# Later weight requests for the last four experts, and other transfer sizes in the order model

## The chip, the core and the metric

The kernel runs on one NeuronCore of one Trainium2 chip. Its time is the device time of one execution in microseconds (us), from launch to end on that core; a time is the median of several executions. The engines are TensorE (PE; its weight loads are PEld), VectorE (DVE), ScalarE (ACT), GpSimd (POOL) and SyncE (SP). SP issues most transfers; POOL issues the indirect ones (gather, scatter) and the casting weight loads of the first three experts.

## The reference, cut to what matters

```python
# stage 1: retention, per batch b and head h (8 x 8, 576 positions, 64 wide)
scores = scale * q @ k.T ;  ret = scores * gamma[h] ** (i - j)   # for j <= i
x = (ret @ v) rearranged to (4608 tokens, 512)
# stage 2: noisy top-2 routing over 8 experts
noisy = x @ w_gate + log1p(exp(x @ w_noise)) * noise
top2, top2_w = the two largest of a token, softmax of the two
# stage 3: experts, 512 -> 1024 -> 512
for e in range(8):
    for k in range(2):
        rows = tokens whose k-th choice is e
        out[rows] += top2_w[rows, k] * (relu(x[rows] @ w1[e]) @ w2[e])
```

## The kernel before

**Staging.** Retention runs over 16 units, four to a pair of batches. When a pair is done, its tokens are routed (`route`), and their x rows, with gates and row numbers behind them, are stored to a DRAM table `xd` (line 1119). An expert's tokens stand in slots, up to 1216 of them (`CAP`), nine tiles of 128 rows and one of 64. A tile whose slots are filled by tokens of the first pairs of batches can be worked on early: `tiles` lists such early tiles (two slots each, `up`, line 1328), which go between the retention work; what is left are 19 late groups of up to four slots (`wide`, lines 1354 and 1418), worked one after the other, experts 0 to 7 in turn.

**One tile.** `fetch` gathers the 128 rows of a slot with one indirect transfer on POOL (line 1246, tile `xg`). Late groups are turned by a transposing transfer on SP (line 1258, `big<-xg`), early ones and those of expert 3 by TensorE (line 1268). Then come w1 (line 1354 or 1328), ReLU on ACT or DVE (lines 1337, 1339), w2 (line 1418; `halves`, line 1437, for the 64-row slot), the gate (lines 1471, 1473) and one or two scatters on POOL (line 1483): the first contribution to a row is written, the second is added in the transfer, or, where rows were read back before (`before`, line 1514, "held"), written too.

**Weights.** Each expert has eight parts of 512 KB: k = 0 to 3 are w1, 4 to 7 are w2. For experts 0 to 2 POOL loads them with a cast. For experts 3 to 7 SP loads each part as f32 into a `big` buffer (`part`, lines 1183 and 1186), and ACT or DVE casts it into the expert's place (lines 459, 461; `W<-big`, for expert 7 `xT<-big`, since it lies where `xT` lay). Experts 4 to 7 take the places of 0 to 3. They are asked for when the last late group of expert e-4 begins. `wide` counts steps, eight to a group; `due` releases the parts whose step has come, in the order in which they were listed, and looks at the head of the list alone.

```python
        for k in range(8):
            self.parts.append((self.step + SPREAD[e] * k, e, k))
```
```python
        while self.parts and self.parts[0][0] <= self.step:
            _, e, k = self.parts.pop(0)
```

**The order.** All operations are first recorded with costs (`pl.op`), and `Plan.run` then writes the order of each engine's instructions by a list schedule: it takes the operation with the earliest estimated start, in buckets of 0.05 us (line 351), then the one with the lower `prio`. The engines run in that order, each waiting on semaphores for real. The argument `dma` of an operation is the estimated occupation of the transfer path in us. It sets when a transfer is taken to have landed; a transfer of POOL also pushes the SP transfers behind it by as much.

```python
                if e == "SP":
                    x += o.dma / 0.95
                else:
                    x += o.dma / 0.85
                    if dma_free.get("SP", 0.0) > t + c:
                        dma_free["SP"] += o.dma
```

Between two indirect transfers of POOL in the estimated stretch from 85 to 200 us, a small memset is put in (line 444). Late gathers are additionally tied to TensorE's progress (`PACE`).

Of the kernel before, what the change touches and what calls it, by code (L numbers as in the profile page):

```python
# [27 lines left out]
NH = E * HPE  # L28
FIRST = (1216, 1024, 855, 690, 526, 361, 197, 0)
WAIT = (10, 15, 15)  # L30
SPREAD = (0, 0, 0, 0, 3, 3, 4, 4)
PACE = 2.343
REST = (85.0, 200.0, 1.6)
AHEAD = (2, 3)
# [379 lines left out]
class Kernel:  # L414
# [736 lines left out]
    def weights(self, e, prio, cast_dma, after=()):  # L1151
# [16 lines left out]
        for k in range(8):  # L1168
            self.parts.append((self.step + SPREAD[e] * k, e, k))
        self.due(prio, after)  # L1170
# [57 lines left out]
    def fetch(self, i, t, prio):  # L1228

        pl, nc = self.pl, self.nc  # L1230
        e, js, early = t
        ident = self.fixed["ident"]
        xi = self.fixed[f"xi{early}"]
        joint = [self.size(j) < P for j in js]
        xg = [self.tailx[e - 1] if two and e % 2 else pl.buf("xg", "exp") for two in joint]
        rows = 1 + 1152 * (early + 1)
        for x, j, two in zip(xg, js, joint):
            if two:
                if e % 2:
                    continue  # L1240
                self.tailx[e] = x
            h, n = HPE * e + j, P
            pace = PACE if early == 3 and i > self.ne else 0.0

            def get(_, x=x, h=h, n=n, pace=pace):
                ins = nc.gpsimd.indirect_dma_start(  # L1246
                    out=x.t[:n, :], out_offset=None, in_=self.xd[:rows, :], in_offset=IOff(ap=xi.t[:n, h:h + 1], axis=0),
                    bounds_check=rows - 1, oob_is_err=False)
                if pace:
                    self.tc.add_manual_dep(ins.ins, self.mm.ins.name, mybir.DependencyInfo(  # L1250
                        mybir.DependencyClass.Sync, mybir.DependencyReason.DATA), reason="gathers go at TensorE's pace")
            self.got = pl.op("POOL", 1.3, get, r=[xi if two else (xi, "m")] + self.xd_done[early], w=[x], prio=prio, dma=0.4, pace=pace, slack=3, ind=True, at="fetch1")
        xT = pl.buf("half" if early < 3 else "big", "xt")
        w, m, off = sum(self.size(j) for j in js), len(js) * P, self.off(js)
        xv = lambda m=m: xT.t.bitcast(BF16)[:, :KD * m].rearrange("p (k s) -> p k s", k=KD)
        if early == 3 and e != 3:
            for s, x in enumerate(xg):
                pl.op("SP", 2.0, lambda _, s=s, x=x, n=self.size(js[s]), p=self.span(e, js[s]): nc.sync.dma_start_transpose(
                    out=xv()[:, :, off[s]:off[s] + n], in_=x.t[p, :DM // 2].bitcast(BF16)),
                    r=[x], w=[(xT, s)], prio=prio, dma=1.1, hold=3, at="fetch2")  # L1260
        for c in range(0, 0 if early == 3 and e != 3 else len(js), 2):
            p = self.psum("xt")
            pv = lambda p=p: p.t.bitcast(BF16).rearrange("p (k s) -> p k s", k=KD)
            for s, x in enumerate(xg[c:c + 2]):
                def tr(_, a=off[c + s] - off[c], x=x, n=self.size(js[c + s]), q=self.span(e, js[c + s]), pv=pv):
                    xb = x.t[q, :DM // 2].bitcast(BF16)
                    for di in range(KD):
                        nc.tensor.transpose(pv()[:, di, a:a + n], xb[:, di * P:(di + 1) * P], ident.t[q, q])  # L1268
                pl.op("PE", 0.25, tr, r=[x, ident], w=[(p, s)], prio=prio, hold=5 if early == 3 else 0, at="fetch3")
            n = sum(self.size(j) for j in js[c:c + 2])  # L1270
            pl.op({"ACT": 0.2 + 0.0032 * n, "DVE": 0.15 + 0.00215 * n}, 0, lambda g, c=c, n=n, pv=pv: self.copy(
                g, xv()[:, :, off[c]:off[c] + n], pv()[:, :, :n]), r=[p], w=[(xT, c)], prio=prio + 2.25, at="fetch4")
        gi = []
        for x, j, two in zip(xg, js, joint):
            k = self.kind(e, j)
            pay = lambda x=x: x.t[:, DM // 2:]
            if early == 3 and two and e % 2 and e < 2:
                c = pl.buf("pay", "exp")
                pl.op("DVE", 0.1, lambda _, x=x, c=c: self.nc.vector.tensor_copy(c.t[:HD], x.t[HD:, DM // 2:DM // 2 + 3]),
                      r=[x], w=[c], prio=prio, hold=3, at="fetch5")  # L1280
                pay, x = (lambda c=c: c.t), c
            if k == "F":
                gi.append((lambda pay=pay: pay()[:, 0:1], lambda pay=pay: pay()[:, 2:3].bitcast(I32), None, x))
            elif k == "S":
                gi.append((lambda pay=pay: pay()[:, 1:2], None, lambda pay=pay: pay()[:, 2:3].bitcast(I32), x))
            else:
                gm, im = self.fix(f"gm{e}", [P, 1]), self.fix(f"im{e}", [P, 2], I32)
                m, mb = self.mix(e)
                V = nc.vector
                pl.op("DVE", 0.17, lambda _, pay=pay, gm=gm: V.tensor_tensor(  # L1290
                    gm.t, pay()[:, 1:2], pay()[:, 0:1], Alu.subtract), r=[x], w=[gm], prio=prio, hold=8, at="fetch6")
                pl.op("DVE", 0.17, lambda _, pay=pay, gm=gm, m=m: V.scalar_tensor_tensor(
                    gm.t, gm.t, m.t[:, 0:1], pay()[:, 0:1], Alu.mult, Alu.add), r=[x, gm, m], w=[gm], prio=prio, hold=8, at="fetch7")
                for y in range(2):
                    pl.op("DVE", 0.17, lambda _, pay=pay, im=im, mb=mb, y=y: V.tensor_tensor(
                        im.t[:, y:y + 1], pay()[:, 2:3].bitcast(I32), mb.t[:, y:y + 1], Alu.add),
                        r=[x, mb], w=[(im, y)], prio=prio, hold=8, at="fetch8")
                gi.append((lambda gm=gm: gm.t[:, 0:1], lambda im=im: im.t[:, 0:1], lambda im=im: im.t[:, 1:2], (gm, im)))
        self.t[i] = dict(xT=xT, xv=xv, gi=gi, w=w)
# [147 lines left out]
    def finish(self, i, t, s, prio, split=False):  # L1447

        pl, nc, tc = self.pl, self.nc, self.tc
        e, js, _ = t  # L1450
        d = self.t[i]
        j = js[s]
        g, first, second, src = d["gi"][s]
        src = list(src) if isinstance(src, tuple) else [src]
        po, n, q = d["po"][s], self.size(j), self.span(e, j, 2)
        y = d.get("y", {}).get(s)
        pair = n < P and e >= 2
        if pair and e % 2:
            y = self.taily[e - 1]
        held = y is not None and (not pair or e >= E - 2)  # L1460
        y = y or pl.buf("half", "exp")
# [29 lines left out]
        if first:  # L1491
            key = self.outk.setdefault(e, pl.fix())
            self.scats.setdefault(i, []).append(pl.op("POOL", 1.3, lambda _: scat(first, False), r=[y] + src, w=[(key, j)],
                                                      prio=prio, dma=0.76, ind=True, at="finish3"))
        if second:
            rd = [self.outk[x] for x in self.outk if x < e]
            self.scats.setdefault(i, []).append(pl.op("POOL", 1.3 if held else 1.8, lambda _: scat(second, not held),
                                                      r=[y] + src + rd, prio=prio, dma=0.9, after=self.reads if held else (), ind=True, at="finish4"))

    def before_it(self, e):  # L1500
        return [w for x in range(e) for w in self.firsts[x]]
# [1 line left out]
    def before(self, i, t, s, prio):  # L1503

        pl, nc, tc = self.pl, self.nc, self.tc
        e, js, _ = t
        q = self.span(e, js[s], 2)
        if self.size(js[s]) < P:
            q, e = slice(0, P), E - 1
        g, first, second, src = self.t[i]["gi"][s]  # L1510
        y = pl.buf("half", "ty")

        def get(_):
            ins = nc.gpsimd.indirect_dma_start(
                out=y.t[q, :], out_offset=None, in_=self.out[:, :], in_offset=IOff(ap=second()[q], axis=0),
                bounds_check=N - 1, oob_is_err=False).ins
            tc.declare_no_dep(ins, group="scat", keep=self.before_it(e), reason="rows of out are disjoint or ordered by hand")
            tc.add_to_no_dep_group("scat", ins)
        self.reads.append(pl.op("POOL", 1.3, get, r=[src] + [self.outk[x] for x in self.outk if x < e], w=[y], prio=prio - 2, dma=0.9))
        self.t[i].setdefault("y", {})[s] = y  # L1520


# [226 lines left out]
```

## Time and profile before

| | us |
|---|---|
| median of 3 runs | 412.27 (411.06 to 412.5) |
| profiled execution, whole | 412.69 |
| its span, first to last instruction | 411.1 |
| PE busy in the span | 377.1 |
| POOL busy | 291.0 |
| ACT busy | 272.3 |
| DVE busy | 148.2 |
| moved by transfers | 98.06 MB, mean 239 GB/s |

The profile is of one execution; times inside it count from the first instruction. In the windows view each row is a stretch, with the busy time and (in brackets) the number of instructions of PE, PEld, DVE, ACT and POOL, the TensorE clock granted (1.00 is full speed), the mean busy share of the 16 transfer engines and GB/s. In the timeline a row is start, duration, engine, line, operation and tiles; the square brackets give the idle time ahead of it and what ended it. A line with a q at the engine is its sequencer.

### The profile page before, as it was taken

To read this page: it belongs to the slowest core of one execution; us is meant where nothing else is said; L and a number is where in the kernel's file an instruction comes from. 1 tells how busy PE (TensorE), PEld (TensorE's weight loads), DVE (VectorE), ACT (ScalarE), POOL (GpSimd) and SP (SyncE) were. 2 spreads that over 40 slices of the span, in tenths; PEclk is the share of its full clock that TensorE was granted. 3 is DMA by queue.
4 is the path that set the end of the run, shared out by engine and by line. 5 is a ranking of instruction groups with operands and counts; after the bars stand their busy time and mean duration, and the time that the engine had idled before them with its cause. 6 is when DMAs were issued, how large, how long until landed. Compare 5 with 4: busy or idle time off the path is not lost.

```text
span 411.1 us, 11031 instructions
## 1 busy us (share of the span) xinstructions
PE 377.1 (92%) x4320; PEld 233.3 (57%) x4320; DVE 148.2 (36%) x413; ACT 272.3 (66%) x468; POOL 291.0 (71%) x379
## 2 busy tenths in 40 slices
PE   4998867889898898999999999999999999999994
PEld 2567656677575666767556554544554454454453
DVE  8456798788269587220111322101011000000002
ACT  2589978898787765776555877666686445555451
POOL 8676783990799848778676477778675776728564
PEclk9899999989999999999999999999999999999999
DMA  8999998999999989999989899999999998839766
GB/s 226 290 298 255 317 305 254 306 269 252 275 286 205 264 188 284 395 246 221 280 188 377 288 331 223 260 251 230 296 257 211 165 202 152 164 45 133 127 94 131
DMA packets 106184, 98.06 MB, mean 239 GB/s; under 512 B 40975, under 2 KB 83472, under 8 KB 106130
## 3 DMA queue, kind: packets, MB, share of 16 engines
q1 hardware_dynamic: 85858, 60.92, 56.0%
q0 software_dynamic: 17584, 36.24, 43.4%
q8 instruction: 34, 0.56, 0.6%
q10 hardware_dynamic: 2688, 0.18, 0.4%
q14 instruction: 20, 0.16, 0.2%
HBM read 73.11 MB, written 26.10 MB: 241 GB/s over the span
## 4 chain that ended last, share of the span: by engine, by line
PE 65%; DVE 8%; POOL 7%; DMA 6%; issue 6%; ACT 6%; POOLq 0%; SPq 0%; another core or an unknown queue 0%; DVEq 0%; ACTq 0%
PE ps L1418 25%; PE ps L1354 23%; PE ps L1328 6%; POOL out_dram L1483 4%; DMA xd<-xg 2%; ACT half L459 2%; DMA half<-in_v_dram 2%; DVE half L783 2%; PE ps L1437 2%; PE ps L808 2%; PE ps L467 1%; POOL half L721 1%; ACT xT L459 1%; DVE olo L1074 1%; PE ps L1268 1%
## 5 line engine op out<-in xcount | busy, mean ns | idle before, releaser
L1337 ACT ACTIVATE half<-ps 128x512 bf16<-128x512 f32 (+5 forms) x184 | 90.6, 503 | 87.5 <-PE ps L1354 55.0
L1418 PE MATMUL ps<-W,half 128*128 128x512 bf16 x432 | 137.8, 379 | 1.4 <-issue 1.1
L1354 PE MATMUL ps<-big,W 128*128 128x512 bf16 (+4 forms) x448 | 124.5, 326 | 0.6 <-DVE half L1473 0.6
L1246 POOL DMA_INDIRECT xg<-xd,xi x76 | 79.1, 1040 | 48.2 <-DMA half<-in_v_dram 11.7
L1483 POOL DMA_INDIRECT out_dram<-half,xg x71 | 90.3, 1272 | 30.1 <-issue 14.8
L1418 PEld LDWEIGHTS <-half 128*128 128x128 bf16 x568 | 54.5, 98 | 62.8 <-issue 3.1
L1354 PEld LDWEIGHTS <-W 128*128 128x128 bf16 x448 | 43.8, 98 | 33.4 <-issue 0.8
L1354 PE MATMUL ps<-big,xT 128*128 128x512 bf16 (+2 forms) x160 | 47.6, 337 | 0.0
L1471 ACT ACTIVATE half<-ps,xg 128x512 f32<-128x512 f32 (+1 forms) x58 | 39.3, 678 | 10.0 <-PE ps L1418 6.7
L783 DVE TENSOR_TENSOR half<-ps,mask 128x512 bf16<-128x512 f32 x64 | 40.3, 682 | 14.3 <-PE ps L775 10.9
L1418 PE MATMUL ps<-xT,half 128*128 128x512 bf16 x136 | 44.9, 379 | 0.0
L459 ACT ACTIVATE half<-ps 128x1024 bf16<-128x1024 bf16 (+1 forms) x42 | 38.5, 946 | 7.9 <-PE ps L744 4.0
L1473 DVE TENSOR_SCALAR half<-ps,xg 128x512 f32<-128x512 f32 (+1 forms) x17 | 10.6, 623 | 76.8 <-PE ps L1437 42.0
L1328 PE MATMUL ps<-half,W 128*128 128x256 bf16 (+1 forms) x288 | 29.1, 255 | 1.6 <-DVE half L461 0.8
L1339 DVE TENSOR_SCALAR half<-ps 128x512 bf16<-128x512 f32 (+5 forms) x12 | 6.8, 569 | 60.5 <-issue 32.9
L1328 PEld LDWEIGHTS <-W 128*128 128x128 bf16 x288 | 23.7, 98 | 5.8 <-issue 1.8
L467 PE MATMUL ps<-mask,ident__61 128*128 128x512 bf16 x68 | 20.3, 429 | 3.7 <-DVE hpf L527 3.7
L1469 DVE SCALAR_TENSOR_TENSOR half<-ps,xg,half 64x256 f32<-64x256 f32 (+2 forms) x7 | 3.6, 521 | 55.2 <-PE ps L1437 32.4
L1354 PEld LDWEIGHTS <-xT 128*128 128x128 bf16 x160 | 15.6, 98 | 12.8 <-issue 0.4
L459 ACT ACTIVATE tb<-ps 64x512 bf16<-64x512 f32 x32 | 18.9, 591 | 4.0 <-POOL half L721 1.9
L459 ACT ACTIVATE W<-big 128x1024 bf16<-128x1024 f32 x20 | 21.0, 1059 | 0.0
L808 PE MATMUL ps<-half,half 64*64 64x64 bf16 (+2 forms) x512 | 17.2, 213 | 1.7 <-ACT xT L459 1.6
(204 smaller groups left out, 517.0 us busy)
## 6 DMA issues: line engine op xcount, KB each, us to landing
big<-in_moe_w_dram SPq DMA_DIRECT2D x40, 512.0 KB
W<-in_moe_w_dram POOLq DMA_DIRECT2D x12, 512.0 KB
xd<-xg SPq DMA_DIRECT2D x16, 264.0 KB
W<-in_q_dram SPq DMA_DIRECT2D x16, 256.0 KB
big<-in_k_dram SPq DMA_DIRECT2D x8, 512.0 KB
big<-in_v_dram SPq DMA_DIRECT2D x8, 512.0 KB
big<-in_q_dram SPq DMA_DIRECT2D x16, 256.0 KB
W<-in_k_dram SPq DMA_DIRECT2D x6, 512.0 KB
```

The costliest lines, as they stand in the source:

```text
L459: self.nc.scalar.activation(out, in_, Act.Copy)
L467: self.nc.tensor.matmul(b.t, lhsT=ident, rhs=mask.rearrange("p r x -> p (r x)").unsqueeze(1).to_broadcast([P, 2, 2 * P]), start=True, stop ...
L783: nc.vector.tensor_tensor(S.t.bitcast(BF16).rearrange("p (h c x) -> p h c x", h=2, c=2)[:, h], p[h].t.rearrange("p (c x) -> p c x", c=2), ...
L808: nc.tensor.matmul(o[h * HD:(h + 1) * HD, hp, n, :], lhsT=kk[:k, r, c, y], rhs=vv[:k, r, c, y].unsqueeze(1).to_broadcast([k, n.stop - n.st ...
L1246: ins = nc.gpsimd.indirect_dma_start(out=x.t[:n, :], out_offset=None, in_=self.xd[:rows, :], in_offset=IOff(ap=xi.t[:n, h:h + 1], axis=0), ...
L1328: nc.tensor.matmul(pv()[:, f2, :], lhsT=w.t[:, o:o + P], rhs=xv()[:, di, :n], start=(di == 0), stop=(di == KD - 1))
L1337: self.nc.scalar.activation(o, i, Act.Relu)
L1354: self.mm = nc.tensor.matmul(p.t[:, :n], lhsT=w.t[:, o:o + P], rhs=xv()[:, di, :n], start=(di == 0), stop=(di == KD - 1))
L1418: self.mm = self.nc.tensor.matmul(po.t, lhsT=hv[:, c:c + P], rhs=self.W[e].t[:, o:o + DM], start=(f == 0), stop=(f == KF - 1))
L1471: nc.scalar.activation(y.t[q, c], x, Act.Copy, scale=g()[q])
L1473: nc.vector.tensor_scalar(y.t[q, c], x, g()[q], None, Alu.mult)
L1483: ins = nc.gpsimd.indirect_dma_start(out=self.out[:, :], out_offset=IOff(ap=ix()[q2], axis=0), in_=y.t[q2, :], in_offset=None, bounds_chec ...
```

## The change

`SPREAD` holds the number of steps between the parts of an expert. It goes from 3, 3, 4, 4 to 5, 6, 7, 8 for experts 4 to 7. Five estimates `dma` change: the gather from 0.4 to 0.3, the transposing transfer from 1.1 to 0.55, the scatter of first contributions from 0.76 to 0.55, the scatter of second contributions from 0.9 to 0.6 where rows were read back and to 1.2 where the transfer adds, the read-back from 0.9 to 0.6. No instruction is added or taken away by hand: the number of memsets between indirect transfers follows from the order.

```diff
-SPREAD = (0, 0, 0, 0, 3, 3, 4, 4)
+SPREAD = (0, 0, 0, 0, 5,6,7,8)
...
-            self.got = pl.op("POOL", 1.3, get, r=[xi if two else (xi, "m")] + self.xd_done[early], w=[x], prio=prio, dma=0.4, pace=pace, slack=3, ind=True, at="fetch1")
+            self.got = pl.op("POOL", 1.3, get, r=[xi if two else (xi, "m")] + self.xd_done[early], w=[x], prio=prio, dma=0.3, pace=pace, slack=3, ind=True, at="fetch1")
...
-                    r=[x], w=[(xT, s)], prio=prio, dma=1.1, hold=3, at="fetch2")
+                    r=[x], w=[(xT, s)], prio=prio, dma=0.55, hold=3, at="fetch2")
...
-                                                      prio=prio, dma=0.76, ind=True, at="finish3"))
+                                                      prio=prio, dma=0.55, ind=True, at="finish3"))
...
-                                                      r=[y] + src + rd, prio=prio, dma=0.9, after=self.reads if held else (), ind=True, at="finish4"))
+                                                      r=[y] + src + rd, prio=prio, dma=0.6 if held else 1.2, after=self.reads if held else (), ind=True, at="finish4"))
...
-        self.reads.append(pl.op("POOL", 1.3, get, r=[src] + [self.outk[x] for x in self.outk if x < e], w=[y], prio=prio - 2, dma=0.9))
+        self.reads.append(pl.op("POOL", 1.3, get, r=[src] + [self.outk[x] for x in self.outk if x < e], w=[y], prio=prio - 2, dma=0.6))
```

## Rows read from the trace of the kernel before

**Rows 1.** The page's parts 1 and 2: PE, then 40 slices of the span.

```profile
PE 377.1 (92%) x4320; PEld 233.3 (57%) x4320; DVE 148.2 (36%) x413; ACT 272.3 (66%) x468; POOL 291.0 (71%) x379
PEclk9899999989999999999999999999999999999999
DMA  8999998999999989999989899999999998839766
```

**Rows 2.** Windows of 20 us, four of the twenty-one.

```profile
100.00:120.00 20.00, 17.70 (x346) 12.94 (x344) 7.73 (x18) 15.78 (x28) 14.14 (x13) 1.00 1.10 290
...
180.00:200.00 20.00, 19.77 (x175) 13.43 (x173) 1.02 (x2) 12.28 (x22) 16.45 (x26) 1.00 0.99 242
...
220.00:240.00 20.00, 19.35 (x150) 11.91 (x148) 5.23 (x13) 14.22 (x26) 12.03 (x12) 1.00 0.93 335
...
380.00:400.00 20.00, 20.00 (x109) 10.09 (x108) 0.45 (x1) 9.91 (x19) 11.50 (x9) 1.00 0.72 108
```

**Rows 3.** Waits of PE from 200 us to the end: total, times, longest.

```profile
PE ps L1354 <- DVE half L1473: 0.6, 1, 0.6
```

**Rows 4.** The timeline around the last matmuls: PE, DVE and POOL.

```profile
403.76 1.92 PE L1427 MATMUL ps<-xT,half 128*128 128x256 bf16 x16
...
405.79 0.48 DVE L1469 SCALAR_TENSOR_TENSOR half<-ps,xg,half 128x256 f32<-128x256 f32 x1 [0.34 <-issue]
...
406.57 0.99 POOL L1483 DMA_INDIRECT out_dram<-half,xg  x1 [0.31 <-issue]
```

**Rows 5.** The timeline of POOL: four gathers, the first of all among them.

```profile
74.34 1.25 POOL L1246 DMA_INDIRECT xg<-xd,xi  x1 [0.17 <-DMA big<-in_q_dram]
...
105.14 1.11 POOL L1246 DMA_INDIRECT xg<-xd,xi  x1 [11.66 <-DMA half<-in_v_dram]
...
133.14 1.08 POOL L1246 DMA_INDIRECT xg<-xd,xi  x1 [0.31 <-issue]
...
149.62 1.08 POOL L1246 DMA_INDIRECT xg<-xd,xi  x1 [0.52 <-issue]
```

**Rows 6.** The timeline of PE: where late groups of experts 0, 4 and 7 begin.

```profile
199.02 0.92 PE L1354 MATMUL ps<-big,W 128*128 128x448 bf16 x4
...
268.57 0.38 PE L1354 MATMUL ps<-big,W 128*128 128x512 bf16 x1
...
369.58 0.38 PE L1354 MATMUL ps<-big,xT 128*128 128x512 bf16 x1
```

**Rows 7.** The timelines of DVE and ACT: first and last of 32 weight casts.

```profile
206.36 1.29 DVE L461 CAST W<-big 128x1024 bf16<-128x1024 f32 x2 [3.52 <-PE ps L1354]
...
315.33 1.05 ACT L459 ACTIVATE xT<-big 128x1024 bf16<-128x1024 f32 x1
```

**Rows 8.** The timeline of SP's queue: its longest piece with weight parts behind it.

```profile
286.83 15.70 SPq L1258 DMA_TRANSPOSE big<-xg  x4
```

**Rows 9.** Groups of POOL by line, 74 to 200 us: count, busy us, mean ns.

```profile
L1246 POOL DMA_INDIRECT xg<-xd,xi x29 | 30.1, 1039 | 20.8 <-DMA half<-in_v_dram 11.7 <-PE ps L1418 4.8 <-issue 3.8
L1483 POOL DMA_INDIRECT out_dram<-half,xg x15 | 15.3, 1021 | 3.3 <-issue 2.7 <-ACT xg L459 0.6
```

**Rows 10.** Windows of 5 us, six of those between 70 and 200 us.

```profile
80.00:85.00 5.00, 3.12 (x88) 2.40 (x86) 4.29 (x25) 4.33 (x8) 4.96 (x6) 0.99 1.10 308
85.00:90.00 5.00, 5.00 (x99) 4.27 (x92) 3.89 (x14) 4.25 (x8) 4.92 (x11) 0.67 1.12 274
...
105.00:110.00 5.00, 3.38 (x48) 2.31 (x47) 0.00 (x0) 4.10 (x6) 4.50 (x5) 1.00 0.98 248
...
130.00:135.00 5.00, 3.95 (x73) 2.08 (x71) 4.43 (x6) 3.00 (x7) 4.52 (x7) 1.00 1.08 237
135.00:140.00 5.00, 3.35 (x104) 2.39 (x101) 3.81 (x5) 3.62 (x6) 4.51 (x6) 1.00 1.19 264
...
160.00:165.00 5.00, 3.89 (x30) 2.12 (x27) 1.75 (x7) 1.58 (x3) 4.45 (x7) 1.00 1.06 391
```

**Rows 11.** Line 1258 from 150 us: durations min, median, max, first and last start.

```profile
L1258 SPq DMA_TRANSPOSE big<-xg x55: 1170/1248/6954, 173.3 to 358.0; - x55
```

## The prediction

> **What bounds the kernel now.** I read the page's first two parts, then the windows, then the waits of PE, and last the timelines of the places where they differ. PE is busy for 92% of the span, and its slices are nearly full in the second half [rows 1]. The windows cut the span into four pieces. Up to the first gather at 74.34 us [rows 5] nothing in the order depends on a changed estimate, so the order is the old one there. From 74.3 to 199.0 us, where the first late group begins [rows 6], retention, routing and early expert tiles share all engines; in the five windows from 100 to 200 us, the first and the last of which are shown, PE stands idle for 2.30 + 3.32 + 0.80 + 1.60 + 0.23 = 8.25 us [rows 2]. From 199 us to the end of the last matmul at 403.76 + 1.92 = 405.7 us PE is full: of ten windows from 200 to 400 us nine show 20.00, one 19.35 [rows 2], and the list of PE's waits has one entry, 0.6 us [rows 3]. Then a tail of 411.1 - 405.7 = 5.4 us follows: the last gating on DVE, one scatter of 0.99 us on POOL, and its landing [rows 4]. So the end is the first 199 us, plus 206.7 us of back-to-back matmuls, plus the tail. The change takes no matmul away. It can win or lose in the 125 us from 74 to 199, and hardly anywhere else.
>
> **Part 1, the weight parts.** The late groups have eight steps each; experts 0 to 3 have 1, 2, 2, 2 of them and the others 3, so experts 4 to 7 begin at steps 56, 80, 104 and 128. The rows give the scale: step 0 at 199.0, step 56 at 268.6, step 128 at 369.6 us [rows 6], so (268.6 - 199.0) / 56 = 1.24 us a step at first and (369.6 - 268.6) / 72 = 1.40 later. Expert 4's parts were asked for at steps 0 to 21, and will be at 0 to 35. The lists of experts 5, 6 and 7 begin at steps 16, 32 and 48, but a part waits until the head of the list goes. So expert 5 now has parts 0 to 3 at step 35, together with expert 4's last, and the rest at 40 to 58 (before: 21 to 37); expert 6 parts 0 to 3 at 58, the rest at 60 to 81 (before: 37 to 60); expert 7 parts 0 to 4 at 81, the rest at 88 to 104 (before: 60 to 76).
> A late part would stop PE, so I price the nearest case. A request takes its way through SP's queue, the transfer and the cast. The longest piece in SP's queue ahead of weight parts is 15.7 us of transposes that wait for gathers [rows 8]. The last of the 32 casts ends at 315.33 + 1.05 = 316.4 us [rows 7]; its request was at step 76, 268.6 + 20 x 1.40 = 296.6 us, so 20 us is the way with that piece on it, and I take 20 for each. Expert 4's last part: 199.0 + 35 x 1.24 + 20 = 262.4 us, used in the second step of its second group (step 65, 281 us). Expert 5's w1: 262.4, used at step 80, 302. Expert 6's w1: step 58, 271.4 + 20 = 291, used at step 104, 336. Expert 7's w1: step 81, 303.6 + 20 = 324, used at 369.6; its last part: step 104, 336 + 20 = 356, used after step 136, 381 us. The smallest margin is 19 us, before it was larger (the last cast was 53 us ahead of expert 7's first matmul).
> What it saves: the casts, 32 of some 1.05 us, mostly on ACT, lie further apart, and SP's transposes find fewer weight parts beside them. PE waits for neither today. So the part is worth 0; its bounds are the only PE wait there, 0.6 us, gained or, where a bunch of casts on ACT holds up a ReLU once, lost.
> The trace thus leaves room for a later request: 316.4 against 369.6 us [rows 6, 7]. The Trainium skill speaks against this edit (DMA: Bandwidth & Descriptors, Rules for kernel authors: issue a transfer early and wait for it late, so that its fixed cost lies beside other work). By that rule the time would grow by whatever a part comes late; with 19 us left it is 0 here too, and the trace agrees as long as no cast comes later than its first matmul.
>
> **Part 2, the estimate of the gather, 0.4 to 0.3, and of first scatters, 0.76 to 0.55.** No instruction changes, only places in the order. From 74 to 200 us POOL issues 29 gathers and 15 scatters [rows 9]. Each gather now pushes SP's estimated landings 0.1 us less, each such scatter 0.21 less, where SP has transfers under way. Order is decided in buckets of 0.05 us, so one gather is enough to swap two instructions. By the three gathers that open later rounds (105.14, 133.14, 149.62 us [rows 5]) 2, 8 and 10 gathers and at the last 4 scatters have gone by: shifts of 0.2, 0.8 and 10 x 0.1 + 4 x 0.21 = 1.84 us. A swap helps when it fills one of PE's holes and costs when it puts an instruction ahead of its transfer in a queue that runs in order. Gain: at most the four largest holes between 105 and 165 us, 1.62 + 1.05 + 1.65 + 1.11 = 5.4 us [rows 10]. Loss: at most each shift waited for on POOL and passed on in full, 0.2 + 0.8 + 1.84 = 2.8 us. Neither end is excluded by a row; I take 0 between them, since PE has other work at hand in most of these windows.
>
> **Part 3, the transposes, 1.1 to 0.55, and the late scatters and read-backs.** The 55 transposes are issued from 173.3 us on [rows 11] and serve the late groups, where PE is full. They are taken to land 0.58 us earlier each, the adding scatters 0.35 us later (0.3 / 0.85), held ones and read-backs 0.35 earlier. POOL and SP are on no PE wait in that piece, so 0, with 0.6 us either way as in part 1. At the end the last scatter follows the last DVE gating directly [rows 4]: nothing to gain; a scatter put in the wrong place ahead of it costs one issue, 0.99 us.
>
> **The sum.** Profiled execution 412.69 = span 411.1 + 1.6 around it. Parts 1, 2 and 3 add 0, so 412.7 for an execution like it; that one lies 0.4 above the median of 412.27. Forecast: 412.3.
>
> **The rivals.**
> *An order that stalls (slower).* The shorter estimates let a gather go on POOL ahead of its stored rows, and retention's multiplies behind it wait, then the matmuls that need them. Such a wait stands in the trace: POOL idle for 11.66 us ahead of the gather at 105.14 [rows 5], with a hole of 1.62 us in PE's window behind it [rows 10]. Against it: the shift there is only 0.2 us. It decides once the shifts of the later rounds reach PE in full, 2.8 us: 412.3 + 2.8 = 415.1. A hole has a second price: after the window from 80 to 85 us, in which PE stood idle for 1.88 us, the next shows a granted clock of 0.67, a mix of the full 2.4 GHz and of 1.2 [rows 10]; 5 us at 0.67 instead of 1.00 lose 1.65 us. One more such window makes 416.8. The Trainium skill (TensorE: Matmul & The Clock Gate, Part 1) says that idleness halves the clock until matmuls have run densely again; the trace agrees in this place, though the holes after 100 us left the clock at 1.00.
> *An order that fills (faster).* Early matmuls come up sooner and close more than half of those four holes, about 3 us: 409.3. For it: in that stretch 8.25 us of PE's time are empty and work for early tiles exists. Against it: the holes are ended by several releasers, not by one late instruction.
> *Transfers in each other's way (hardly faster).* If thinner weight traffic were the gain, it would have to show in PE from 200 us on: at most 0.6 us, 411.7. This lies within no change.
> *The change doesn't do what it says.* The head of the list holds the parts back, so four or five come together at steps 35, 58 and 81 and w1 is not spread at all. With the margins above this costs nothing: 412.3.
>
> **How the numbers follow.** A measurement of this kernel can tell about 0.5%, 2.1 us, from no change. Forecast with parts 1 and 3 at 0 and part 2 within 2 us: 0.36; the change not spreading: 0.05; thinner traffic: 0.03; together no change, 0.44. The order that stalls: 0.30, at 414.4 to 417. The order that fills: 0.26, at 407 to 410.2. The predicted time is the likeliest's, 412.3. For 8 in 10 the range goes down to 408.6, past the filling rival's 409.3 and short of the full 5.4, and up to 416.8, the stalling rival with its clock.
>
> **What the profile would show.** Part 1 is right if the casts reach to about 350 us and PE's waits after 200 us stay near 0.6; wrong if PE waits for a cast or an ACT instruction there. Part 2 is right if POOL's timeline is the same up to 74 us and the first late group begins within 2 us of 199.0; it is wrong by as much as that start moves. Part 3 is right if the piece from there to the last matmul is 206.7 us long again, and the tail 5.4. The prediction fails if a single swap delays routing and so every tile behind it, or if retention ends earlier and PE's holes close together.

## The result

On the chip of the first measurement the changed kernel takes 420.42 us in the median of 20 runs (412.43 to 424.8), the kernel before 411.74 (408.19 to 413.22). The ratio given with the result compares, for each kernel, the executions close to its fastest (within about 1.5%), and is 1.011, 95% interval 1.0072 to 1.0148; the changed kernel's times spread so far that its plain median stands 2.1% above. Slower, then: by 1.1 to 2.1%. On a second chip, with the kernel before on the same chip, the ratio was 1.0248 (1.019 to 1.0306).

The profiled execution of the changed kernel took 424.57 us, one of its longest, with a span of 422.9. Where the span grew, in 20 us windows (columns as in [rows 2]):

```profile
core 0: us, PE busy (x) PEld busy (x) DVE busy (x) ACT busy (x) POOL busy (x), PEclk, DMA share, GB/s
...
100.00:120.00 20.00, 19.47 (x406) 15.08 (x405) 7.34 (x15) 17.85 (x31) 13.34 (x12) 0.99 1.14 293
...
180.00:200.00 20.00, 19.49 (x169) 12.97 (x167) 2.07 (x4) 11.73 (x21) 17.08 (x26) 1.00 0.96 241
...
220.00:240.00 20.00, 20.00 (x152) 12.40 (x151) 3.05 (x9) 15.38 (x28) 13.49 (x14) 1.00 0.89 282
...
300.00:320.00 20.00, 17.92 (x90) 8.12 (x88) 2.98 (x8) 10.88 (x18) 12.73 (x11) 0.91 1.07 274
320.00:340.00 20.00, 13.02 (x62) 5.89 (x60) 0.00 (x0) 9.26 (x16) 8.34 (x8) 0.89 1.20 200
340.00:360.00 20.00, 20.00 (x113) 10.24 (x112) 0.97 (x2) 11.42 (x21) 12.68 (x11) 0.94 0.92 174
```

The stretch before the late groups is no longer than it was: from 100 to 200 us PE's idle time is 3.88 us in the five windows together (two of them shown), against 8.25, while from 60 to 100 us it is 10.10 against 8.04. The hole is between 300 and 340 us, where PE had none before, and the granted clock is below 1.00 there too. The first late group and the last matmuls:

```profile
197.97 0.92 PE L1354 MATMUL ps<-big,W 128*128 128x448 bf16 x4
...
415.16 1.92 PE L1427 MATMUL ps<-xT,half 128*128 128x256 bf16 x16
```

Against [rows 6] the late groups begin 1.05 us earlier; against [rows 4] they end 11.4 us later. The late piece is 415.16 + 1.92 - 197.97 = 219.1 us long, 12.4 more than the 206.7 of before. The waits of PE and of ACT in it (PE's answer to [rows 3]):

```profile
PE ps L1418 <- ACT half L1337: 7.0, 2, 3.5
PE ps L1354 <- ACT half L1337: 2.1, 1, 2.1
...
ACT xT L459 <- DMA big<-in_moe_w_dram: 12.5, 5, 7.4
ACT W L459 <- DMA big<-in_moe_w_dram: 6.9, 2, 6.7
```

PE waits 9.1 us for ReLUs on ACT (line 1337), and ACT waits 19.4 us for weight parts (line 459). Before, PE waited 0.6 us there [rows 3], so 8.5 of the 12.4 us are new waits. The rest, 3.9 us, fits the lower clock: at 0.91, 0.89 and 0.94 the three windows from 300 to 360 us would lose 20 x (0.09 + 0.11 + 0.06) = 5.2 us if PE were busy all through them, which is an upper estimate. In the timelines of ACT and PE both waits stand side by side:

```profile
299.10 0.68 ACT L1471 ACTIVATE half<-ps,xg 128x512 f32<-128x512 f32 x1
306.50 1.06 ACT L459 ACTIVATE W<-big 128x1024 bf16<-128x1024 f32 x1 [6.73 <-DMA big<-in_moe_w_dram]
307.47 0.53 ACT L1337 ACTIVATE half<-ps 128x192 bf16<-128x192 f32 x2
...
324.27 0.61 ACT L1337 ACTIVATE half<-ps 128x512 bf16<-128x512 f32 x1
332.32 1.06 ACT L459 ACTIVATE xT<-big 128x1024 bf16<-128x1024 f32 x1 [7.44 <-DMA big<-in_moe_w_dram]
333.28 0.58 ACT L1337 ACTIVATE half<-ps 128x512 bf16<-128x512 f32 x1
...
336.33 1.06 ACT L459 ACTIVATE xT<-big 128x1024 bf16<-128x1024 f32 x1 [1.90 <-DMA big<-in_moe_w_dram]
...
307.83 0.38 PE L1354 MATMUL ps<-big,W 128*128 128x512 bf16 x1 [2.08 <-ACT half L1337]
...
333.91 0.39 PE L1418 MATMUL ps<-W,half 128*128 128x512 bf16 x1 [3.43 <-ACT half L1337]
...
337.93 0.61 PE L1418 MATMUL ps<-W,half 128*128 128x512 bf16 x1 [3.54 <-ACT half L1337]
```

In ACT's written order the cast at 306.50 stands ahead of ReLUs. Its part has not landed, and ACT does nothing for 6.73 us, while the results of finished matmuls wait for their ReLUs; PE runs out of ReLUs and stops until 307.83. The same happens at 332.32 and, with a shorter wait, at 336.33. The weights themselves are in time: experts 6 and 7 need these casts tens of us later. SP's queue shows why the parts are late:

```profile
282.04 12.85 SPq L1258 DMA_TRANSPOSE big<-xg  x4
294.98 0.53 SPq L1186 DMA_DIRECT2D big<-in_moe_w_dram  x1
295.61 2.96 SPq L1258 DMA_TRANSPOSE big<-xg  x2
298.66 0.54 SPq L1186 DMA_DIRECT2D big<-in_moe_w_dram  x1
299.29 4.49 SPq L1183 DMA_DIRECT2D big<-in_moe_w_dram  x4
306.56 12.71 SPq L1258 DMA_TRANSPOSE big<-xg  x3
319.36 0.53 SPq L1186 DMA_DIRECT2D big<-in_moe_w_dram  x1
```

In the list of SP's waits from 200 us on, the largest entry is that of the transposes for their gathers:

```profile
SPq L1258 <- DMA xg<-xd,xi: 55.2, 19, 7.2
```

Transposes hold SP for 12.85 us and for 12.71 us, and the parts are issued behind them. Before, a piece of 15.70 us stood in that queue [rows 8], and ACT waited for no part: new is where the casts stand. And a part that is issued does not land at once: by the order of the two queues, the part issued at 294.98 is the one that the cast at 306.50 waits for, 11.5 us, and that of 319.36 the one of the cast at 332.32, 13 us. In the order model a part's estimate is 1.35 / 0.95 + 2.16 = 3.6 us from issue to landing, and more only if the model has other transfers ahead of it.

### The profile page after: what moved, and what is told of

Its sections match the earlier page's. It is cut to its first block, busy times and chain, and to the rows that moved or that the text cites. A ratio compares the mean times of both kernels' runs of the same rounds, so it can differ in the third digit from the quotient of the medians.

```text
span 422.9 us, 11023 instructions
## 1 busy us (share of the span) xinstructions
PE 382.2 (90%) x4319; PEld 238.5 (56%) x4319; DVE 146.8 (35%) x410; ACT 275.5 (65%) x471; POOL 289.2 (68%) x376
## 5 line engine op out<-in xcount | busy, mean ns | idle before, releaser
L1418 PE MATMUL ps<-W,half 128*128 128x512 bf16 x432 | 140.2, 384 | 7.0 <-ACT half L1337 7.0
L1354 PE MATMUL ps<-big,W 128*128 128x512 bf16 (+4 forms) x448 | 127.1, 332 | 2.1 <-ACT half L1337 2.1
L1471 ACT ACTIVATE half<-ps,xg 128x512 f32<-128x512 f32 x58 | 39.7, 685 | 12.3 <-PE ps L1418 11.4
L783 DVE TENSOR_TENSOR half<-ps,mask 128x512 bf16<-128x512 f32 x64 | 40.3, 683 | 17.4 <-PE ps L775 13.6
L1473 DVE TENSOR_SCALAR half<-ps,xg 64x256 f32<-64x256 f32 (+1 forms) x17 | 10.1, 593 | 88.2 <-PE ps L1437 40.5
L459 ACT ACTIVATE W<-big 128x1024 bf16<-128x1024 f32 x22 | 23.1, 1053 | 7.0 <-DMA big<-in_moe_w_dram 6.9
L459 ACT ACTIVATE xT<-big 128x1024 bf16<-128x1024 f32 x16 | 16.7, 1054 | 13.1 <-DMA big<-in_moe_w_dram 13.0
L459 ACT ACTIVATE xg<-ps 128x1024 bf16<-128x1024 bf16 (+1 forms) x19 | 17.3, 940 | 6.3 <-PE ps L1110 5.4
```

The lines of the kernel that those rows point to most:

```text
L459: self.nc.scalar.activation(out, in_, Act.Copy)
L783: nc.vector.tensor_tensor(S.t.bitcast(BF16).rearrange("p (h c x) -> p h c x", h=2, c=2)[:, h], p[h].t.rearrange("p (c x) -> p c x", c=2), ...
L1354: self.mm = nc.tensor.matmul(p.t[:, :n], lhsT=w.t[:, o:o + P], rhs=xv()[:, di, :n], start=(di == 0), stop=(di == KD - 1))
L1418: self.mm = self.nc.tensor.matmul(po.t, lhsT=hv[:, c:c + P], rhs=self.W[e].t[:, o:o + DM], start=(f == 0), stop=(f == KF - 1))
L1471: nc.scalar.activation(y.t[q, c], x, Act.Copy, scale=g()[q])
L1473: nc.vector.tensor_scalar(y.t[q, c], x, g()[q], None, Alu.mult)
```

## Experiments

Theory C, made from this profile: a cast in ACT's order ahead of its part is what PE pays for. Its rival E: the hole comes with the order of the early stretch, or with this chip. All ratios are to the kernel before on the same chip; its median was 418.36 on the first of the three chips used, 410.95 on the second, 420.06 on the third, so times of different chips are not set against each other. Ratios of different chips are no close comparison either: the kernel after itself had 1.011 on one and 1.0248 on another. The first four runs were on the first chip.

**The new `SPREAD` alone.**

```diff
 # kernel before
-SPREAD = (0, 0, 0, 0, 3, 3, 4, 4)
+SPREAD = (0, 0, 0, 0, 5,6,7,8)
```

> The kernel before with the new SPREAD and the old estimates. Theory C (casts: a weight part asked for later stands in SP's queue behind transposes that wait for gathers, its cast stands in ACT's queue ahead of the ReLUs, and PE waits for these): slower than before by 2 to 9 us, with ACT waiting on DMA at line 459 for several us after 280 us and PE waiting for ACT line 1337. Theory E (the estimates alone make the difference, by the order of the stretch from 74 to 199 us): within 1 us of before, no such wait.

Ratio 1.0009 (0.998 to 1.0038): no change. No PE wait at all is listed after 199 us, no wait of ACT on a part, and the late piece is 205.6 us long. Theory C as written is wrong: later requests alone do not put a cast ahead of its part. Its chain of waits stays possible, with another start.

**The estimates alone.**

```diff
 # kernel after
-SPREAD = (0, 0, 0, 0, 5,6,7,8)
+SPREAD = (0, 0, 0, 0, 3, 3, 4, 4)
```

> The kernel after with the old SPREAD (3, 3, 4, 4). Theory C: the late piece is 207 us long again with under 1 us of PE waits, and the first late group begins about 1 us before 199.0 as in the profile after: 0 to 2 us faster than before. Theory E: slower than before by the 4 us or so that the changed kernel lost.

Ratio 0.9974 (0.9929 to 1.002). But in the waits of PE and ACT of this kernel, the old `SPREAD` notwithstanding:

```profile
PE ps L1354 <- ACT half L1337: 2.5, 1, 2.5
PE ps L1418 <- ACT half L1337: 1.2, 2, 0.9
...
ACT xT L459 <- DMA big<-in_moe_w_dram: 14.2, 4, 5.6
ACT W L459 <- DMA big<-in_moe_w_dram: 2.7, 2, 1.7
```

The late piece is 410.60 + 1.92 - 199.25 = 213.3 us. The estimates bring the waits, which neither theory said together with a level ratio. The twelve times reach from 414.05 to 425.55 us, and their median, 421.39, is 0.7% above that of the kernel before. Whether something else in the estimates gains is not shown by this run.

**The casts later in the order.**

```diff
 # kernel after, in part()
-        pl.op({"ACT": 1.06, "DVE": 0.7}, 0, lambda g: self.copy(g, w.t[:, k * F:(k + 1) * F], t.t), hold=1,
+        pl.op({"ACT": 1.06, "DVE": 0.7}, 0, lambda g: self.copy(g, w.t[:, k * F:(k + 1) * F], t.t), hold=14,
```

> The kernel after, but the order takes a weight part's cast for possible 14 us after its landing (hold 14 in place of 1), so that it stands later in ACT's queue; the requests are as in the kernel after. Theory C: ACT no longer waits on DMA at line 459, PE's waits after 200 us fall from 9 us to under 2, and the time is 411 to 413. If the late transfers themselves were the cause (a part that lands after its first matmul), PE would wait on the casts instead and nothing is won.

Ratio 1.0148 (1.01 to 1.0196): against the expectation, and not what was meant to be tried. The edit also holds for the casts of expert 3, which are loaded ahead of the others; PE lost 7.5 us in the one window from 200 to 220 us, and the late groups began at 210.81. In the late piece, 418.92 + 1.92 - 210.81 = 210.0 us, the waits are fewer but not gone: from 210.8 us on PE waits 2.5 us for ReLUs on ACT, and ACT 8.2 us for parts. So 14 us of room in the model did not keep every cast behind its part here. The time tells nothing of the cause; the run with expert 3 left out of the edit stands below.

**The casts of experts 4 to 7 on DVE.**

```diff
 # kernel after, in part()
-        pl.op({"ACT": 1.06, "DVE": 0.7}, 0, lambda g: self.copy(g, w.t[:, k * F:(k + 1) * F], t.t), hold=1,
+        pl.op({"ACT": 1.06, "DVE": 0.7} if e < 4 else {"DVE": 0.7}, 0, lambda g: self.copy(g, w.t[:, k * F:(k + 1) * F], t.t), hold=1,
```

> The kernel after, with the casts of experts 4 to 7 on DVE alone, which is idle for over 85% of that piece. Theory C: a cast that waits for its part then holds up no ReLU on ACT; PE's waits after 200 us fall under 2 us and the time is 410 to 413. What could go on: DVE holds ReLUs and gatings too, which then wait behind the cast (PE waits for DVE lines 1339 or 1473).

Ratio 0.9904 (0.9865 to 0.9944). The thirteen times reach from 412.36 to 426.67 us, with a median of 417.12 against 418.36. The profile is of the longest: there DVE waits 88 us for parts, and PE 3.2 us for DVE's gating (line 1473) and 3.6 us for a transpose, where under 2 us had been expected. So in that execution the stall moved to another engine, and most of it cost PE nothing. What the shorter ones waited for is not known.

**The estimate of the transposes alone** (this and the next three on the second chip). Theory T: the transposes' 0.55 makes the order model take SP's queue for shorter than it is. Rival S: the estimates of gathers and scatters do it.

```diff
 # kernel before, in fetch()
-                    r=[x], w=[(xT, s)], prio=prio, dma=1.1, hold=3, at="fetch2")
+                    r=[x], w=[(xT, s)], prio=prio, dma=0.55, hold=3, at="fetch2")
```

> The kernel before with one change: the estimate of the transposing transfer 0.55 in place of 1.1. The order up to the late groups is that of before. Theory T (this one estimate makes the order model take SP's queue for shorter than it is, so that casts go into ACT's queue ahead of their parts): ACT waits on DMA at line 459 for 5 us or more, PE for ACT in the late piece for 2 us or more, and the time is 1 to 5 us above before. Theory S (the estimates of gathers and scatters do it): as before within 1 us and no such wait.

Ratio 1.018 (1.0128 to 1.0232), from five executions: one number makes the kernel slower. The order up to the late groups is that of before. Waits in the profiled execution, which at 411.45 us is the shortest of the five (the others 416 to 421):

```profile
PE ps L1418 <- ACT half L1337: 1.7, 1, 1.7
PE ps L1437 <- ACT half L1337: 0.8, 1, 0.8
...
ACT xT L459 <- DMA big<-in_moe_w_dram: 13.2, 4, 6.2
```

Its late piece is 402.40 + 1.92 - 195.77 = 208.6 us, 3.0 more than in the run with the new `SPREAD` alone. The waits are shown by this, but not all of the 1.8%: no profile of a longer execution of this kernel exists.

**The kernel after with the transposes at 1.1** (called transposes_old below)**.**

```diff
 # kernel after, in fetch()
-                    r=[x], w=[(xT, s)], prio=prio, dma=0.55, hold=3, at="fetch2")
+                    r=[x], w=[(xT, s)], prio=prio, dma=1.1, hold=3, at="fetch2")
```

> The kernel after, with the estimate of the transposing transfer back at 1.1; SPREAD and the other estimates as in the kernel after. Theory T: PE's waits in the late piece fall under 1 us, and what is left is the gain of the order in the stretch from 74 to 199 us: 0 to 4 us faster than before. Theory S: the waits of 9 us stay.

Ratio 0.9945 (0.9916 to 0.9974). All other parts of the change are in it, `SPREAD` too, and it is faster than before. PE has no wait after 199 us, ACT waits for one part, and the late piece is 400.93 + 1.92 - 197.26 = 205.6 us:

```profile
197.26 0.92 PE L1354 MATMUL ps<-big,W 128*128 128x448 bf16 x4
...
400.93 1.92 PE L1427 MATMUL ps<-xT,half 128*128 128x256 bf16 x16
...
ACT xT L459 <- DMA big<-in_moe_w_dram: 0.8, 1, 0.8
```

Theory T holds, and S falls: gathers and scatters at their new estimates make PE wait for nothing.

**The estimates of gathers, scatters and read-backs alone.**

```diff
 # kernel after
-SPREAD = (0, 0, 0, 0, 5,6,7,8)
+SPREAD = (0, 0, 0, 0, 3, 3, 4, 4)
...
-                    r=[x], w=[(xT, s)], prio=prio, dma=0.55, hold=3, at="fetch2")
+                    r=[x], w=[(xT, s)], prio=prio, dma=1.1, hold=3, at="fetch2")
```

> The kernel before with the new estimates of gathers, scatters and read-backs alone (transposes 1.1, SPREAD 3, 3, 4, 4). Theory T: no wait of PE for casts, and the early order of the kernel after: 1 to 4 us faster than before. Theory S: ACT waits on casts as in the run with the estimates alone.

Ratio 0.9982 (0.9947 to 1.0017), no PE wait, late piece 205.6 us. ACT does wait 7.1 us for parts, in eight waits of at most 1.3 us; short waits on ACT cost PE nothing here. The expected gain is not beyond doubt here, and it overlaps with the run before it: whether `SPREAD` helps once the transposes are at 1.1 stays open.

**The kernel after once more.**

> The kernel after, on the same chip as these. By theories T and S alike 1.011 of before, with PE waits in the late piece of 5 to 10 us; a ratio of 1.00 would say that the first measurement was of that chip.

Ratio 1.0248 (1.019 to 1.0306). PE waits 8.2 us for ACT, ACT 17.4 for parts; the late piece is 215.8 us. The loss is no matter of the chip of the first measurement. Nor are the waits a matter of one long execution: this profile is of 419.29 us, where the five lie between 418.35 and 424.45.

**The casts of experts 4 to 7 later** (this and the last three on the third chip).

```diff
 # kernel after, in part()
-        pl.op({"ACT": 1.06, "DVE": 0.7}, 0, lambda g: self.copy(g, w.t[:, k * F:(k + 1) * F], t.t), hold=1,
+        pl.op({"ACT": 1.06, "DVE": 0.7}, 0, lambda g: self.copy(g, w.t[:, k * F:(k + 1) * F], t.t), hold=1 if e < 4 else 14,
```

> The kernel after, all its estimates and its SPREAD, but the casts of experts 4 to 7 alone are taken for possible 14 us after landing (hold 14 in place of 1); the early casts of expert 3 keep their place. Theory T: the place of the casts in ACT's queue is the cause; ACT's waits on DMA at line 459 fall under 3 us, PE's in the late piece under 1.5 us, and the time is 0.99 to 1.00 of before. If the waits go to other places (transposes, or PE waiting for a cast), the late requests themselves are to blame and the time stays above 1.01.

Ratio 0.987 (0.9797 to 0.9942), where the kernel after had 1.011 and 1.0248 on other chips. The five times reach from 412.68 to 427.50 us, with a median of 415.83 against 420.06, so the size of the gain is not firm. All estimates and the late requests are as in the kernel after; the late casts alone stand further back, all 32 of them on ACT. The waits of PE after 199 us, complete:

```profile
PE ps L1418 <- issue: 0.3, 1, 0.3
PE ps L1418 <- ACT half L1337: 0.2, 1, 0.2
```

ACT has no wait on a part, and the late piece is 206.2 us. So the place of the casts in ACT's order is the cause of the waits, and in this profile the later weights cost nothing.

**The gather's estimate alone.**

```diff
 # kernel before, in fetch()
-            self.got = pl.op("POOL", 1.3, get, r=[xi if two else (xi, "m")] + self.xd_done[early], w=[x], prio=prio, dma=0.4, pace=pace, slack=3, ind=True, at="fetch1")
+            self.got = pl.op("POOL", 1.3, get, r=[xi if two else (xi, "m")] + self.xd_done[early], w=[x], prio=prio, dma=0.3, pace=pace, slack=3, ind=True, at="fetch1")
```

> The kernel before with the gather's estimate alone at 0.3. Theory O (what is gained comes from the order of the stretch from 74 to 199 us, which this estimate already changes at the same instruction of PE as the whole change): 0 to 2.5 us faster than before, late piece within 1.5 us of 205.6. If the scatters' estimates do it: as before within 1 us.

Ratio 0.9899 (0.9857 to 0.994), the late piece 404.61 + 1.92 - 200.02 = 206.5 us. It is as long as before, so what this number gains should lie ahead of the late groups. That is argued: no profile of the kernel before on this chip exists, and all four kernels tried on it came out 1.0 to 1.5% below, so that the kernel before may just have been slow there. In PE's order it moves the same first instruction as the whole change does: four transposes of an early tile (line 1268) come in between retention's matmuls of line 775, earlier than they did.

**Requests that are really spread.**

```diff
 # kernel after with the transposes at 1.1, in weights()
-        self.due(prio, after)
+        self.parts.sort(); self.due(prio, after)
```

> As the run transposes_old, with the list of due parts sorted by step, so that each expert's parts really come 5, 6, 7 or 8 steps apart and none waits for the head of the list. If bunched requests cost something: up to 1 us faster than transposes_old, 0.990 to 0.9945 of before. If they cost nothing: 0.9945 within 0.003. A late piece of 205.6 us without PE waits is the floor, and no more than that can come from it.

Ratio 0.9899 (0.9828 to 0.997), with a median of six of 418.93 against 420.06; and the waits are back: ACT 11.7 us for parts, PE 3.5 us for ACT, a late piece of 210.1 us. With the bunches (transposes_old) there were none, so it is not the bunches that bring the waits. Sorting asks for every part at its own step, so for the w1 of experts 5 to 7 earlier than with the bunches; why casts then stand ahead of their parts again is open.

**A little room for each cast.**

```diff
 # kernel after with the transposes at 1.1, in part()
-        pl.op({"ACT": 1.06, "DVE": 0.7}, 0, lambda g: self.copy(g, w.t[:, k * F:(k + 1) * F], t.t), hold=1,
+        pl.op({"ACT": 1.06, "DVE": 0.7}, 0, lambda g: self.copy(g, w.t[:, k * F:(k + 1) * F], t.t), hold=1 if e < 4 else 4,
```

> As the run transposes_old, with casts of experts 4 to 7 taken for possible 4 us after landing in place of 1. In the profile of transposes_old ACT waited 0.8 us on a part and PE for nothing, so 0.9945 of before within 0.003; if executions without a profile lose time to such waits now and then, it is faster by up to 1 us and its runs lie closer together.

Ratio 0.9855 (0.9812 to 0.9898), the fastest on its chip by the median, 414.30 against 420.06; no wait of PE after 199 us, none of ACT on a part, late piece 205.6 us. This version beats the kernel before. Against the kernel after, which was not run on this chip, only the ratios speak, 0.9855 against 1.011 and 1.0248.

## Why the prediction was right and wrong

The measured time lies in the range when the ratio 1.011 is taken (411.7 x 1.011 = 416.3, range 408.6 to 416.8); the plain median, 420.4, does not. The likeliest case, no change, did not come about, and the slower time came by a mechanism that was not the slower rival's. So it is luck that the range holds 416.3: its upper end was made from a stall on POOL that did not happen.

- *What bounds the kernel: right, in the main.* The late piece is matmuls back to back and has a floor: 205.6 us in four kernels with the one `SPREAD` or the other and several sets of estimates. "Hardly anywhere else" was wrong: a piece with nothing to gain had 9 us to lose.
- *Part 1, `SPREAD`: right by itself, for half of the reason given.* 0 was forecast and 1.0009 measured. The margins held: no kernel shows PE waiting on a late weight part in the late piece, but for 0.6 us for a cast in the kernel with the list sorted. The step that failed is the next sentence: that PE waits for neither, "so the part is worth 0", bounds 0.6 us. I priced a cast that comes too late for its matmul. I did not price a cast that stands too early in an in-order queue, and what is queued behind it; the bunch of casts on ACT was named, at 0.6 us where the profile shows 9.1. The sum also takes the parts as independent, and they may not be: PE's waits for ACT are 0 with the new `SPREAD` alone, 4.0 us with the estimates alone, and 9.1 and 8.2 with both, in single profiles.
- *Part 3, the transposes: the step that failed.* It gave 0 with 0.6 us either way, since POOL and SP were on no PE wait. But the estimate does not act on the transposes alone: it sets when the model takes the weight parts behind them in SP's queue for landed, and with that the place of their casts. Alone it has a ratio of 1.018, and back at 1.1 it takes the kernel after to 0.9945 without any PE wait. The 20 us from request to cast that I had read from [rows 7, 8] was the warning: the model allows 3.6 us from issue to landing for a part with nothing ahead of it. The old 1.1 was too long for one transpose, if the new figures are right, and too short for the queue's real waits; it had left room by accident. That last sentence is a reading, not a measurement.
- *Part 2, the early order: the right mechanism, on the other side of 0.* 0 was taken between -5.4 and +2.8. The gather's estimate alone has a ratio of 0.9899, some 4 us of 420.06, and from 100 to 200 us the kernel after loses less to holes (3.88 against 8.25 us), though it begins the late groups only 1.05 us earlier. The filling rival thus seems to have come true in this part and to have been outweighed; that is argued. How large the gain is differs by kernel and chip (0.9982 with all the small estimates on the second chip), and single profiles can't settle it: with the same early order the late groups began at 199.02 in the kernel before, at 195.77 in that with the transposes' estimate alone and at 207.21 in that with the new `SPREAD` alone.
- *The stalling rival: right sign, wrong place.* It put a gather ahead of its rows on POOL between 105 and 150 us, at 2.8 us. What happened is the same mistake on ACT, with weight parts, at 300 to 340 us. The row that it leant on names a load of `in_v` as what ended POOL's 11.66 us, not stored rows. Its second price was right in kind: the clock in the windows behind the new holes was 0.89 and 0.94.
- *No spreading at all: half right.* The head of the list does bunch the parts; no run shows a cost of that, and sorting the list brought waits.

## What to carry to other kernels

In an order written from estimates, an instruction that waits for a transfer is dangerous in two directions; ask of each in-order queue not only whether the data come in time for their use but what stands behind the instruction if they come late. An estimate made truer for one transfer, if 0.55 is that, can make the whole model worse where its error had covered for another: check the waits of the instructions that follow the transfers behind it in the queue. Where a consumer has tens of microseconds to spare, place it late: here that one number took the waits out of the changed kernel, and its ratio from 1.011 and 1.025 on two chips to 0.987 on a third.

## What had not been expected of the hardware

The two weight parts of 512 KB followed above took 11.5 and 13 us from issue to landing beside gathers and transposes (the page's median for such parts, where it could tell, is 10.0 us), with the transfer engines at a share of 1.07 to 1.20 in those windows. The same kernel before had medians of 411.74, 418.36, 410.95 and 420.06 us in four sessions, and as far as single profiles tell, the late piece, where PE is full, hardly took part in that: the kernel with the new `SPREAD` alone, in a session with 418.36, needs 205.6 us for it and begins it at 207.21 us. In late holes the clock fell: with 7.0 us of idle time in the window from 320 to 340 us it was granted at 0.89, a mix of its two levels of 1.2 and 2.4 GHz, and at 0.94 in the next, in which PE did not stop.
